# Spreading the auxiliary matmuls of a transformer block over its score units, with zero products in the idle TensorE time, a leaner prologue and tail, and softmax sums inverted in a 128x16 tile

## The chip, the cores and the metric

The kernel runs on one core of one Trainium2 chip. The metric is the device time of one execution in microseconds (us). A profiled execution also has a "span", from its first to its last instruction, which is about 2 us shorter than its time.

A core has five engines that matter here. TensorE (PE in the profile) multiplies matrices and writes to PSUM, of which the kernel uses eight banks of 512 fp32 columns. ScalarE (ACT) does the exponentials, VectorE (DVE) and GpSimd (POOL) do elementwise work, and SyncE (SP) issues most DMA transfers. Each engine runs its own list of instructions in order, and engines wait for each other by semaphores.

## The reference, cut to what matters

The computation is one block: a modulated layernorm, attention with 32 heads, a second modulated layernorm, and an MLP that begins with a layernorm of its own. S = 2048 rows, D = 640, head dimension 20, F = 1536, bf16.

```python
mod = (_silu(c) @ w_mod).reshape(c.shape[0], 6, 1, -1)      # sa, ca, ga, sb, cb, gb
h = _layernorm(x) * (1 + ca) + sa
    q, k, v = ...(h @ wqkv)                                  # 32 heads of 20
    scores = einsum('bhqd,bhkd->bhqk', q, k) * Dh ** (-0.5)
    p = softmax(scores)                                      # 32 x 2048 x 2048 exponentials
    o = einsum('bhqk,bhkd->bhqd', p, v)
x = x + ga * (o @ wo)
h = _layernorm(x) * (1 + cb) + sb
    y = _layernorm(h)
    h = _gelu(einsum('bsd,df->bsf', y, w1) + b1)
    ... einsum('bsf,fd->bsd', h, w2) + b2
x = x + gb * (...)
```

The 134 million exponentials are what bounds the kernel: at 128 lanes they are 694 ACT instructions, 661 of them 128x1536.

## The kernel before

The kernel is a Python program that lists operations, and a small list scheduler inside it that decides the order on each engine. The scheduler has a model of time (`dur`, `lat`, a DMA bandwidth). It chooses the operation that is ready first by this model, and by priority among those that are ready. The order is then fixed in the program: on the chip nothing is reordered.

The query rows are cut in four chunks of 512, the heads in 8 groups of 4. One "score unit" is three score matmuls into three PSUM banks, and one exp over them. Units alternate between banks 0 to 2 and 3 to 5; bank 6 takes the products with V. So **one bank, number 7, is left for everything else** in the steady part: projections of later groups, softmax sums, output projection and MLP of the previous chunk. I call these auxiliary matmuls.

```python
def score_unit(ts, b0, prio=1):            # three matmuls into banks b0..b0+2, then one exp
    ...
    P.op("pe", em, R=R, W=[pb], ..., prio=prio, mode="r", name="qk")
    acts.append(P.op("act", lambda e: e.activation(dst, src, ACTF.Exp, scale=SCALE), ...))   # L587

def proj_job(g, which, tc, prio, rel, eng):
    bb = bank(aux_bank())
    for kt in range(KD):                   # all five become available at the same exp, `rel`
        mm(bb, wqk[:, kt, which, ...], hT[:, kt, ...], kt == 0, kt == KD - 1, prio, 512, rel=rel, name="proj")
    ...

def sel_job(qc, g, rel, prio=6):           # softmax sums of a group of four heads
    bb = bank(aux_bank())
    d = ot[:, qc % 2, g, :]
    mm(bb, selz, d, True, True, prio, 512, rel=rel, name="sel")       # row of sums -> all rows of its head
    dve(lambda e: e.reciprocal(rinv, bb), [bb], [rinv], 512, ...)     # L616, 128x512
    dve(lambda e: e.tensor_tensor(d, d, rinv, op=ALU.mult), ...)      # L617

# prologue
dve(lambda e: e.memset(wqk, 0.0), [], [wqk], KD * 2 * NG * 128, mode=2)     # L441
dve(lambda e: e.memset(va_flat, 1.0), [], [va_flat], TT * H * VW, mode=2)   # L442
...                                        # four steps of 512 rows: layernorm, transpose, project, all of V,
...                                        # and the scores of head group 0
row_mod(gab, wm1, 0, None); row_mod(sbr, wm1, D, None); ...                 # then row modulations and wo scaling
# tail, per 128 rows
normalize(hdst, x2[:, tl, :], tt, 3)
dve(lambda e: e.tensor_tensor(hdst, hdst, cb1, op=ALU.mult), ..., eng=eng)  # eng = "pool", L820
dve(lambda e: e.tensor_tensor(hdst, hdst, sbr, op=ALU.add), ..., eng=eng)   # L822
```

The softmax here doesn't subtract the row's maximum and nothing guards it: scores larger than these inputs give would overflow.

Of the kernel before, what the change touches and what calls it, by code (L numbers as in the profile page):

```python
# [6 lines left out]
ALU = mybir.AluOpType  # L7
# [6 lines left out]
class Op:  # L14
    __slots__ = ("eng", "emit", "strong", "weak", "dur", "lat", "prio", "rel", "idx",
                 "users", "dma", "nbytes", "name", "npred", "ready", "t0", "t1",
                 "inc", "cnt", "sem", "startusers", "mode", "order")


class Sched:  # L20
# [7 lines left out]
    NDSEM = 40  # L28

    def __init__(self, nc, es):  # L30
        self.nc = nc
        self.ops = []
        self.lw = {}
        self.rd = {}
        self.fp = {}
        self.sem = {e: es.enter_context(nc.semaphore("s_" + e))
                    for e in ("pe", "act", "dve", "pool")}
        self.dsem = [es.enter_context(nc.semaphore(f"dm{i}")) for i in range(self.NDSEM)]
        self.ndma = 0
        self.dlast = [None] * self.NDSEM  # L40
# [35 lines left out]
    def op(self, eng, emit, R=(), W=(), dur=0.1, lat=None, prio=5, rel=None, name="",  # L76
           dma=False, nbytes=0, mode=0, after=()):
        o = Op()
        o.eng, o.emit, o.dur, o.prio, o.rel, o.name = eng, emit, dur, prio, rel, name
        o.lat = dur if lat is None else lat  # L80
        o.dma, o.nbytes, o.mode = dma, nbytes, mode
        o.idx = len(self.ops)
# [37 lines left out]
    def schedule(self):  # L120
# [4 lines left out]
        for o in ops:  # L125
            for i in o.strong | o.weak:
                ops[i].users.append(o.idx)
                o.npred += 1
            if o.rel is not None:
                o.rel.startusers.append(o.idx)  # L130
                o.npred += 1
# [5 lines left out]
        bw = 0.0  # L137
        for o in ops:
            if o.npred == 0:
                avail[o.eng].append(o)  # L140
        left = len(ops)
        while left:
# [6 lines left out]
            assert be is not None, "deadlock"  # L149
            cand = [x for x in avail[be] if x.ready <= bt + 1e-9]  # L150
# [4 lines left out]
            if be == "pe" and lastmode[be] != o.mode:  # L155
                d += 0.05
                lastmode[be] = o.mode
            free[be] = bt + d
            if o.dma:
                s = max(bt + 1.4, bw)  # L160
                bw = s + o.nbytes / 260e3
                o.t1 = bw + 0.8
            else:
                o.t1 = bt + (d - o.dur) + o.lat
# [98 lines left out]
def bass_adaLN_cond__mha_block__mixer_channel_mlp__prompt_kernel(  # L263
# [6 lines left out]
    NG, TT, NQC, KD, KF = 8, 16, 4, 5, 12  # L270
# [3 lines left out]
    VW, RING = 24, 15  # L274

    es = ExitStack()
    with es:
# [28 lines left out]
        o_qT = alloc(NQC * NG * 512 * 2)  # L306
# [9 lines left out]
        qT = V(o_qT, [NQC, NG, 512])  # L316
# [5 lines left out]
        ring = V(o_ring, [RING, 512])  # L322
# [11 lines left out]
        raw = V(o_qT + 8192, [KD, 3 * D])  # L334
        wm0 = V(o_ring, [KD, 2 * D])
        wm1 = V(o_qT + 8192, [KD, 2 * D])
        wm2 = V(o_kT + 4 * S * 2, [KD, 2 * D])
        xb = [V(o_wo, [4, D]), V(o_wo + 5120, [4, D]), V(o_mlp, [4, D])]
        hn1 = V(o_kT + 2 * S * 2, [6, D])
        ident = V(alloc(256), [128])  # L340
        selz = V(alloc(256), [128])
        rinv = V(alloc(2048), [512], F32)
        gbb2 = V(alloc(1280), [D])
        sbr = V(alloc(1280), [D])
        cb1 = V(alloc(1280), [D])
        gbh = V(o_mlp + 5120, [D])
        gab = V(o_mlp + 6400, [D])
        b2b = V(o_kT + S * 2, [D])
        st6 = [V(alloc(64), [2, 6], F32) for _ in range(6)]
        st2 = V(alloc(TT * 64), [TT, 16], F32)  # L350
        c_row = V(alloc(256), [128])
        b1row = V(alloc(256), [128])
        small = V(alloc(64), [16], F32)
# [6 lines left out]
        sbl = V(o_kT + S * 2 + 1280, [KD, 128])  # L360
        ones = V(o_kT + S * 2 + 2560, [128])
# [6 lines left out]


        def c_pe(n):  # L370
            return n / 2400.0

        def act(outp, inp, func, R=(), W=None, n=512, prio=5, name="", **kw):
            d = n / 1200.0 + 0.082
            return P.op("act", lambda e: e.activation(outp, inp, func, **kw),  # L375
                        R=[inp] + list(R), W=[outp], dur=d, lat=d + 0.22, prio=prio, name=name)

        def dve(emit, R, W, n, mode=1.0, prio=5, name="", extra=0.0, eng="dve"):
            d = 0.06 + n / (960.0 * mode) + extra
            if eng == "pool":  # L380
                d = 0.1 + n / 800.0 + extra
            return P.op(eng, emit, R=R, W=W, dur=d, lat=d + 0.12, prio=prio, name=name)

        def dma(eng, o_, i_, nbytes, prio=5, name=""):
            return P.op(eng, lambda e: e.dma_start(o_, i_), R=[i_], W=[o_], dur=0.6 if eng != "pool" else 1.0,
                        dma=True, nbytes=nbytes, prio=prio, name=name)

        def mm(outp, lhsT, rhs, start, stop, prio, n, mode="f", rel=None, tp=None, name="", R=None):
            kw = {} if tp is None else dict(tile_position=tp)
            return P.op("pe", lambda e: e.matmul(outp, lhsT, rhs, start=start, stop=stop, **kw),  # L390
                        R=[lhsT, rhs] if R is None else R, W=[outp], dur=c_pe(max(n, 64)),
                        lat=c_pe(max(n, 64)) + 0.15, prio=prio, mode=mode, rel=rel, name=name)

        def tr(outp, inp, idn, prio, n=128, rel=None, name=""):
            return P.op("pe", lambda e: e.transpose(outp, inp, idn), R=[inp, idn], W=[outp],  # L395
                        dur=c_pe(n), lat=c_pe(n) + 0.15, prio=prio, mode="f", rel=rel, name=name)

        banks = [[0, 1, 2, 3, 4, 5, 6, 7], 0]
# [8 lines left out]


# [3 lines left out]
        def xsrc(tc):  # L412
            return X2[tc * 512:(tc + 1) * 512, :].rearrange("(t p) d -> p t d", p=128)

        cv = c[0]
        dma("sp", c_row[0:KD, :], cv.rearrange("(kt p) -> kt p", p=128), 1280)
        dma("sp", xb[0][:, 0:2, :], xsrc(0)[:, 0:2, :], 327680)
        dma("sp", xb[0][:, 2:4, :], xsrc(0)[:, 2:4, :], 327680)
        dma("act", wm0[:, :, 0:D], wmod_v[:, :, 0:D], 819200, prio=0)
        dma("act", wm0[:, :, D:2 * D], wmod_v[:, :, D:2 * D], 819200, prio=0)  # L420
        dma("sp", raw[:, :, D:2 * D], wqkv_v[:, :, D:2 * D], 819200)
        dma("sp", raw[:, :, 0:D], wqkv_v[:, :, 0:D], 819200)
        dma("sp", wv[:], wqkv_v[:, :, 2 * D:3 * D], 819200)
        dma("sp", xb[1][:], xsrc(1), 655360)
        dma("sp", xb[2][:], xsrc(2), 655360)
# [4 lines left out]
        def pool(emit, W, n, R=(), prio=5, name=""):  # L430
            return dve(emit, list(R), list(W), n, prio=prio, name=name, eng="pool")

        pool(lambda e: e.memset(ident, 0.0), [ident], 128)
        pool(lambda e: e.affine_select(out=ident, in_=ident, compare_op=ALU.not_equal, fill=1.0,
                                       base=0, pattern=[[-1, 128]], channel_multiplier=1),
             [ident], 128, R=[ident])
        pool(lambda e: e.memset(ones, 1.0), [ones], 128)
        pool(lambda e: e.memset(negh, -0.5), [negh], 16)
        wqk_k = wqk[:, :, 1, :]
        wqk_q = wqk[:, :, 0, :]  # L440
        dve(lambda e: e.memset(wqk, 0.0), [], [wqk], KD * 2 * NG * 128, mode=2)  # L441
        dve(lambda e: e.memset(va_flat, 1.0), [], [va_flat], TT * H * VW, mode=2)  # L442


        b = aux_bank()
        tb = bankh(b)
        tr(tb[:, 0:KD], c_row[0:KD, :], ident[0:KD, 0:KD], 0, 16)
        act(t_col, tb[:, 0:KD], ACTF.Tanh, n=KD, scale=0.5, prio=0)
        dve(lambda e: e.tensor_copy(c_col, tb[:, 0:KD]), [tb[:, 0:KD]], [c_col], KD, prio=0)
        dve(lambda e: e.tensor_scalar(t_col, t_col, 0.5, 0.5, op0=ALU.mult, op1=ALU.add),  # L450
            [t_col], [t_col], KD, prio=0)
        dve(lambda e: e.tensor_tensor(s_col, t_col, c_col, op=ALU.mult), [t_col, c_col], [s_col], KD, prio=0)  # L452

        def mod_cols(wm, base, blocks, prio, rel=None):

            bb = bank(aux_bank())
            for m in blocks:
                for kt in range(KD):
                    mm(bb[:, m:m + 1], wm[:, kt, (m - base) * 128:(m - base + 1) * 128],
                       s_col[:, kt:kt + 1], kt == 0, kt == KD - 1, prio, 100, rel=rel)  # L460
            m0, m1 = blocks[0], blocks[-1] + 1
            dve(lambda e: e.tensor_copy(modc[:, m0:m1], bb[:, m0:m1]), [bb[:, m0:m1]], [modc[:, m0:m1]],
                m1 - m0, prio=0)

        mod_cols(wm0, 0, list(range(0, 10)), 0)
        dve(lambda e: e.tensor_scalar_add(modc[:, 5:10], modc[:, 5:10], 1.0), [modc[:, 5:10]],
            [modc[:, 5:10]], 5, prio=0)


        def pad_copy(which, kt, eng):  # L470
            dst = wqk[:, kt, which, :].rearrange("p (h i) -> p h i", i=32)[:, :, 0:DH]
            src = raw[:, kt, which * D:(which + 1) * D].rearrange("p (h i) -> p h i", i=DH)
            if eng == "act":
                act(dst, src, ACTF.Copy, n=D, prio=3)
            else:
                dve(lambda e: e.tensor_copy(dst, src), [src], [dst], D, eng=eng, prio=6)

        for kt in range(KD):
            pad_copy(1, kt, "act" if kt % 2 == 0 else "pool")
        for kt in range(KD):  # L480
            pad_copy(0, kt, "act" if kt % 2 == 0 else "pool")


        def stats(xt, tt, si, prio):
            s6 = st6[si]
            s2 = st2[:, tt, 0:2]
            for hf in range(2):
                xi = xt[:, hf * 320:(hf + 1) * 320]
                dve(lambda e, hf=hf, xi=xi: e.bn_stats(s6[:, hf, :], xi), [xi], [s6[:, hf, :]], 400, prio=prio)  # L489
            dve(lambda e: e.bn_aggr(s2, s6), [s6], [s2], 30, extra=0.06, prio=prio)  # L490

        def rstd(t0, n, prio):
            v = st2[:, t0:t0 + n, 1]
            r = st2[:, t0:t0 + n, 2]
            pool(lambda e: e.tensor_scalar_add(r, v, 1e-5), [r], 4, R=[v], prio=prio)  # L495
# [474 lines left out]
```

## Time and profile before

| | before |
|---|---|
| median time | 1132.8 us |
| span of the profiled execution | 1127.9 us |
| ACT busy | 977.9 us, of which exp 933.2 |
| first exp / first 1536-wide exp | 33.3 / 97.9 us |
| last exp ends | 1058.8 us |
| mean granted TensorE clock | 0.796 |

First some lines of the page: the busy time of each engine (share of the span, number of instructions), the granted TensorE clock in 40 equal slices (tenths of full speed), the chain of work that ended last (shares of the span), and three groups of instructions (busy us, mean ns of one, then idle time of the engine just before them and what ended most of it).

```profile
PE 864.7 (77%) x5675; PEld 263.7 (23%) x5740; DVE 414.6 (37%) x577; ACT 977.9 (87%) x766; POOL 138.7 (12%) x165
...
PEclk9998999899577687578678776588667687688759
...
ACT 59%; PE 30%; DVE 6%; POOL 4%; issue 1%; another core or an unknown queue 0%; POOLq 0%; DVEq 0%
...
L587 ACT ACTIVATE arena<-psum 128x1536 bf16<-128x1536 f32 (+2 forms) x694 | 933.2, 1481 | 64.3 <-PE psum L578 63.4
...
L390 PE MATMUL psum<-arena 128*128 128x320 bf16 (+2 forms) x1417 | 353.3, 378 | 49.6 <-DVE arena L452 17.3
...
L616 DVE RECIPROCAL arena<-psum 128x512 f32<-128x512 f32 x32 | 107.4, 3355 | 20.1 <-PE psum L578 15.3
```

ACT bounds the kernel, and PE is the only engine it really waits for. The 128x512 reciprocals take 3.36 us each on DVE.

Next the ACT timeline: start, length in us, the instruction and how many in a row, and in brackets the idle time before it and what ended that.

```profile
33.32 1.94 ACT L587 ACTIVATE arena<-psum 128x1024 bf16<-128x1024 f32 x2 [0.20 <-PE psum L578]
...
97.88 2.79 ACT L587 ACTIVATE arena<-psum 128x1536 bf16<-128x1536 f32 x2 [17.64 <-PE psum L578]
101.09 1.45 ACT L587 ACTIVATE arena<-psum 128x1536 bf16<-128x1536 f32 x1 [0.41 <-PE psum L578]
103.76 1.45 ACT L587 ACTIVATE arena<-psum 128x1536 bf16<-128x1536 f32 x1 [1.22 <-PE psum L578]
...
107.79 45.89 ACT L587 ACTIVATE arena<-psum 128x1536 bf16<-128x1536 f32 x34 [0.95 <-PE psum L578]
...
1097.41 1.02 ACT L375 ACTIVATE arena<-psum 128x1024 bf16<-128x1024 bf16 x1 [38.56 <-PE psum L395]
```

Where nothing is missing, 34 exps take 45.89 us, so 1.35 us each (1.347 from one start to the next). The 661 exps of this size and 18 tanh of 0.94 us make about 907 us, which no part of this change touches. The rest of the 1128 us lies in the prologue (the 17.64 us gap, and five exps that limp up to 107.8), in waits of the steady part, and in the tail (the 38.56 us gap and the MLP after it).

The waits of ACT for score matmuls between 125 and 1035 us (total, number, longest, in us), and the granted clock (the column after POOL) in stretches of 141 us:

```profile
ACT arena L587 <- PE psum L578: 41.0, 68, 1.5
```

```profile
141.00:282.00 141.00, 120.39 (x823) 34.00 (x839) 53.05 (x59) 139.37 (x104) 0.00 (x0) 0.98 0.02 6
282.00:423.00 141.00, 108.44 (x697) 28.43 (x705) 53.33 (x75) 133.75 (x100) 39.80 (x40) 0.70 0.08 28
```

In the first whole stretch PE has 120 us of work and is granted 0.98; from 282 us on it has about 108 and is granted 0.70 to 0.77. The Trainium skill, "TensorE: Matmul & The Clock Gate", Part 1, describes this: by default the clock is throttled to half, and activity over windows of 3413 ns releases it. The trace agrees: its clock records from 32 us on hold only 1.0 and 0.5, all but the last in multiples of 3.413 us, so that a figure like 0.70 is a mean of full and half clock. So the fullest stretch for PE runs it the fastest. (The first 141 us, with 103 us of work and 0.96, are no counterexample: the first 32 us, in which PE does little, have no clock record and count as full.)

### The profile page before, as it was taken

How to read it: one execution, taken by the hardware profiler on the slowest of the kernel's cores; microseconds unless marked ns; L12 is line 12 of the kernel's file. 1: busy time of each engine (PE TensorE's matmuls, PEld its weight loads, DVE VectorE, ACT ScalarE, POOL GpSimd, SP SyncE). 2: the span in 40 equal slices, each digit the busy share in tenths (PEclk: the TensorE clock that was granted, in tenths of full speed). 3: DMA queues.
4: the chain of work that ended last, by engine and by line, in shares of the span. 5: the costliest groups of instructions: out<-in, count | busy, mean ns of one | idle time of the engine just before them, and what ended most of it. 6: DMA issues, size and time to landing. Idle time of an engine off the chain costs nothing.

```text
span 1127.9 us, 13029 instructions
## 1 busy us (share of the span) xinstructions
PE 864.7 (77%) x5675; PEld 263.7 (23%) x5740; DVE 414.6 (37%) x577; ACT 977.9 (87%) x766; POOL 138.7 (12%) x165
## 2 busy tenths in 40 slices
PE   1997888888787768777787777877787877777818
PEld 1442222222122211122222211122122211122305
DVE  8722434333234354322034444322233444322361
ACT  2874999999999999999999998999989999999502
POOL 2124000000524100000024100000025000000080
PEclk9998999899577687578678776588667687688759
DMA  8110000000300000000000000000000000000000
GB/s 287 75 30 1 1 1 1 24 2 2 139 1 1 1 1 1 24 6 12 6 1 1 1 1 1 24 11 8 6 1 1 1 1 1 24 12 6 6 1 24
DMA packets 14259, 20.99 MB, mean 19 GB/s; under 512 B 634, under 2 KB 12282, under 8 KB 14202
## 3 DMA queue, kind: packets, MB, share of 16 engines
q1 hardware_dynamic: 12890, 18.52, 4.9%
q10 hardware_dynamic: 1312, 1.64, 0.5%
q8 instruction: 45, 0.74, 0.3%
q14 instruction: 12, 0.10, 0.0%
HBM read 17.54 MB, written 2.62 MB: 18 GB/s over the span
## 4 chain that ended last, share of the span: by engine, by line
ACT 59%; PE 30%; DVE 6%; POOL 4%; issue 1%; another core or an unknown queue 0%; POOLq 0%; DVEq 0%
ACT arena L587 57%; PE psum L390 16%; PE psum L578 8%; PE psum L603 5%; DVE arena L616 1%; ACT arena L375 1%; DVE arena L442 1%; PE psum L395 1%; POOL arena L787 1%; POOL arena L820 1%; POOL arena L827 1%; DVE arena L489 1%; POOL arena L822 1%; POOL arena L496 1%; DVE arena L809 0%
## 5 line engine op out<-in xcount | busy, mean ns | idle before, releaser
L587 ACT ACTIVATE arena<-psum 128x1536 bf16<-128x1536 f32 (+2 forms) x694 | 933.2, 1481 | 64.3 <-PE psum L578 63.4
L578 PE MATMUL psum<-arena 32*128 32x512 bf16 x2048 | 321.5, 463 | 175.6 <-ACT arena L587 170.1
L390 PE MATMUL psum<-arena 128*128 128x320 bf16 (+2 forms) x1417 | 353.3, 378 | 49.6 <-DVE arena L452 17.3
L603 PE MATMUL psum<-arena 128*32 128x512 bf16 x2048 | 247.0, 473 | 3.7 <-DVE arena L610 3.7
L390 PEld LDWEIGHTS psum<-arena 128*128 128x128 bf16 x1482 | 128.7, 107 | 230.7 <-issue 118.8
L578 PEld LDWEIGHTS psum<-arena 32*128 32x128 bf16 x2048 | 68.5, 93 | 428.1 <-ACT arena L587 352.7
L616 DVE RECIPROCAL arena<-psum 128x512 f32<-128x512 f32 x32 | 107.4, 3355 | 20.1 <-PE psum L578 15.3
L495 POOL TENSOR_SCALAR arena<-arena 128x1 f32<-128x1 f32 (+1 forms) x40 | 10.1, 252 | 710.5 <-DVE arena L490 710.1
L603 PEld LDWEIGHTS psum<-arena 128*32 128x32 bf16 x2048 | 54.2, 96 | 161.8 <-issue 151.2
L540 DVE CAST arena<-psum 128x512 bf16<-128x512 f32 x60 | 41.5, 691 | 117.7 <-PE psum L390 114.5
L875 DVE SCALAR_TENSOR_TENSOR arena<-psum,arena 128x320 bf16<-128x320 f32 x32 | 15.7, 492 | 182.7 <-PE psum L390 182.6
L847 DVE TENSOR_SCALAR arena<-psum,arena 128x512 bf16<-128x512 f32 x36 | 27.0, 751 | 101.4 <-PE psum L390 101.4
L610 DVE CAST arena<-psum 128x512 bf16<-128x512 f32 x32 | 22.0, 688 | 101.0 <-PE psum L603 100.9
L375 ACT ACTIVATE arena<-psum 128x320 bf16<-128x320 f32 (+3 forms) x22 | 10.7, 496 | 44.4 <-PE psum L395 38.6
L489 DVE BATCH_NORM_STATS2 arena<-arena 128x6 f32<-128x320 bf16 x96 | 43.5, 481 | 15.2 <-POOL arena L822 14.4
L395 PE MATMUL psum<-arena 128*128 128x128 bf16 (+2 forms) x162 | 19.3, 271 | 31.5 <-DVE arena L499 28.1
L809 DVE TENSOR_TENSOR arena<-psum,arena 128x320 bf16<-128x320 f32 x32 | 15.1, 489 | 75.2 <-PE psum L390 75.1
L888 POOL TENSOR_TENSOR arena<-arena 128x640 bf16<-128x640 bf16 x12 | 16.3, 1400 | 197.7 <-DMA arena<-in_B_w_dram 197.7
L499 DVE TENSOR_SCALAR arena<-arena 128x640 bf16<-128x640 bf16 x48 | 27.3, 584 | 25.3 <-POOL arena L496 25.2
L375 ACT ACTIVATE arena<-arena 128x1024 bf16<-128x1024 bf16 (+1 forms) x24 | 23.8, 1007 | 8.9 <-DMA arena<-in_A_wqkv_dram 8.9
L375 ACT ACTIVATE arena<-psum,arena 128x512 bf16<-128x512 bf16 (+1 forms) x24 | 17.3, 741 | 15.5 <-PE psum L395 10.7
L858 DVE SCALAR_TENSOR_TENSOR arena<-arena 128x1024 bf16<-128x1024 bf16 x18 | 21.9, 1217 | 22.6 <-ACT arena L375 22.4
(42 smaller groups left out, 232.5 us busy)
## 6 DMA issues: line engine op xcount, KB each, us to landing
arena<-in_A_x_dram SPq DMA_DIRECT2D x7, 640.0 KB, 4.2
arena<-in_B_w_dram SPq DMA_DIRECT2D x2, 1920.0 KB, 10.2
arena<-in_w_mod_dram SPq DMA_DIRECT2D x2, 1600.0 KB, 10.2
out_dram<-arena SPq DMA_DIRECT2D x16, 160.0 KB, 1.8
arena<-in_A_wqkv_dram SPq DMA_DIRECT2D x3, 800.0 KB, 11.2
arena<-in_w_mod_dram ACTq DMA_DIRECT2D x2, 800.0 KB, 7.2
arena<-in_A_wo_dram SPq DMA_DIRECT2D x4, 200.0 KB
arena<-in_A_x_dram SPq DMA_DIRECT2D x2, 320.0 KB, 6.5
```

The lines of the kernel that those rows point to most:

```text
L375: return P.op("act", lambda e: e.activation(outp, inp, func, **kw), R=[inp] + list(R), W=[outp], dur=d, lat=d + 0.22, prio=prio, name=name)
L390: return P.op("pe", lambda e: e.matmul(outp, lhsT, rhs, start=start, stop=stop, **kw), R=[lhsT, rhs] if R is None else R, W=[outp], dur=c_ ...
L395: return P.op("pe", lambda e: e.transpose(outp, inp, idn), R=[inp, idn], W=[outp], dur=c_pe(n), lat=c_pe(n) + 0.15, prio=prio, mode="f", r ...
L489: dve(lambda e, hf=hf, xi=xi: e.bn_stats(s6[:, hf, :], xi), [xi], [s6[:, hf, :]], 400, prio=prio)
L499: dve(lambda e: e.tensor_scalar(dst, xt, st2[:, tt, 0:1], st2[:, tt, 2:3], op0=ALU.subtract, op1=ALU.mult), [xt, st2[:, tt, 0:3]], [dst], ...
L540: dve(lambda e: e.tensor_copy(d, bb), [bb], [d], 512, prio=2)
L578: r = e.matmul(o_, lh, rh, start=True, stop=True, tile_position=(32 * hl, 0))
L587: acts.append(P.op("act", lambda e: e.activation(dst, src, ACTF.Exp, scale=SCALE), R=[pb], W=[dst], dur=d, lat=d + 0.24, prio=4, name="exp"))
L603: r = e.matmul(o_, lh, rh, start=(kt == 0), stop=(kt == TT - 1), tile_position=(0, 32 * hl))
L610: dve(lambda e: e.tensor_copy(d, bank(6)), [bank(6)], [d], 512, prio=0, name="pvcopy")
L616: dve(lambda e: e.reciprocal(rinv, bb), [bb], [rinv], 512, extra=2.8, prio=3, name="recip")
L847: dve(lambda e: e.tensor_scalar(d, bb, b1col[:, ft:ft + 1], None, op0=ALU.add), [bb, b1col], [d], 512, prio=2, name="m1ev")
```

## The change

The intent has four parts.

1. **Prologue.** The memsets touch only what has to be set; the q and k weights of head group 0 are loaded first; only a quarter of V is made, and the rest of V and the row modulations move under the exps of chunk 0.
2. **Steady part.** The matmuls of one auxiliary job become available one by one, at different score units (`Pace`). The scheduler also inserts zero products (zero weights, added to bank 6 where they change nothing) where its model of PE is idle and has streamed fewer than 3500 columns in the last 3.413 us.
3. **Softmax sums.** The 4x512 sums of a group go by DMA into a 128x16 tile, are inverted there, go to DRAM and come back as a broadcast. This replaces 31 of the 32 large reciprocals.
4. **Tail.** The second layernorm runs on ACT and DVE instead of POOL, and most of the output projection is summed before the last group is ready.

The diff also retunes the scheduler's own model: the assumed DMA rate goes from 260 to 350 GB/s, and PE's assumed time now doubles after a window with little PE work.

The diff, cut to its core:

```diff
+            if be == "pe" and self.filler is not None and gate and bt > free["pe"] + 0.06:
+                f0 = free["pe"]
+                while fl and fl[0][0] < f0 - self.TICK:      # TICK = 3.413
+                    fl.pop(0)
+                if sum(x[1] for x in fl) < self.fill_min:    # fill_min = 3500 columns
+                    o = self.op("pe", self.filler[0], ..., name="fill", wc=float(self.filler[1]))
...
+        P.filler = (lambda e: e.matmul(bank(6), zero, idr, start=False, stop=False, ...), 512)
...
+            def rels(self, n):                               # class Pace
+                return [self.u0 + int(self.slot + self.span * i / n) for i in range(n)]
...
-            for kt in range(KD):
-                mm(bb, wqk[...], hT[...], kt == 0, kt == KD - 1, prio, 512, rel=rel, name="proj")
+            mmjob(bb, [(wqk[...], hT[...]) for kt in range(KD)], 512, prio, pace, "proj")
...
+        def sum_job(ci, g):
+            P.op("sp", lambda e: e.dma_start(dst, row), R=[d], W=[sumt], ..., nbytes=4096)       # L716
+            dve(lambda e: e.reciprocal(r_, s_), [s_], [r_], 16, dur=0.2, prio=3, name="recip")   # L718
+            o = P.op("sp", lambda e: e.dma_start(flat_, r_), R=[r_], ..., nbytes=8192)           # L720
+            src = bass.AP(tensor=scr.tensor, offset=k * 2048, ap=[[n, 4], [0, 32], [1, n]])
+            P.op("sp", lambda e: e.dma_start(rb, src), W=[rb], ..., nbytes=262144, after=[o])    # L723
+            dve(lambda e: e.tensor_tensor(d, d, rb, op=ALU.mult), [d, rb], [d], n, ..., name="div")  # L724
...
-        dve(lambda e: e.memset(wqk, 0.0), [], [wqk], KD * 2 * NG * 128, mode=2)
-        dve(lambda e: e.memset(va_flat, 1.0), [], [va_flat], TT * H * VW, mode=2)
+        pool(lambda e: e.memset(wqk32[:, :, 10:16], 0.0), ...)
+        dve(lambda e: e.memset(va32[:, :, 10:12], 1.001937866210937500), ...)
...
-        pool(lambda e: e.memset(wo_pad, 0.0), [wo_pad], NG * D)
+        pool(lambda e: e.memset(wo_pad, 0.0), [wo_pad], dur=4.4, prio=7)                         # L868, runs at 29.65 us; in the old kernel at 57.2
...
-            ln2(pq, tl)
+            ln2(ci, tl, tail=True)             # normalize on ACT, products on DVE
+        early = [(tl, half) for tl in range(min(nt, 3)) for half in range(2)]
```

## The prediction

It was written from the reference, the code before, the diff and the profile before, with nothing built.

> **What bounds it now.** The exp activations of L587 on ACT. By groups they are busy 933 of 1127.9 us; the chain gives ACT 59%. The ACT timeline shows the pace when nothing is missing: 32 exps of 128x1536 in 43.2 us, 1.35 us each. 661 of them make about 890 us and 18 tanh in between (0.94 us each) 17 us: 907 us that this change does not touch. The rest, about 221 us, is what can shrink:
> - Prologue: the first exp starts at 33.3 us (DVE spent 14.6 us on two memsets before its first statistics at 19.0). Head group 0 lasts to 80.2 with PE 93 to 99% busy. Then ACT idles 17.6 us while the row modulations and the wo scaling run, and limps until 107.8, having done 5 large exps.
> - Steady part: ACT waited 41 us for score matmuls (68 waits between 125 and 1035 us). The granted clock is 0.98 at 141 to 282 us, then 0.70 to 0.77. The waits follow runs of 3 to 8 auxiliary matmuls of 0.33 to 0.43 us each in front of a score unit.
> - Tail: 69 us from the last exp's end (1058.9). The second layernorm, with 12 POOL products of 1.39 us in the chain, holds the MLP back to 1098.
>
> **What the change does.**
> 1. Prologue: smaller memsets, q/k weights of group 0 loaded first, only a quarter of V made there, row modulations and the rest of V moved under the exps. First exp at about 19 us; each of the four steps falls from about 12 us to about 10.3 (then ACT, 9.7 us of work); group 1 follows at once. The steady part starts near 60 instead of an effective 101 (107.8 less 5 exps): -41 us.
> 2. Steady part: auxiliary matmuls come one at a time, and zero products keep PE active. The Trainium skill, "TensorE: Matmul & The Clock Gate", Part 1, says activity releases the clock; the trace agrees so far, as the densest stretch had 0.98. I expect over 0.93 throughout, and PE waits of ACT near 10 us, not 41. The first chunk takes on V and row work; its second group is the tight one.
> 3. Softmax sums: 31 of 32 reciprocals (3.36 us each) leave DVE, but three DMAs in sequence replace each. The broadcast's outer dimension of 4 limits it to 4 DMA engines by the skill's "DMA: Bandwidth & Descriptors", Rules for kernel authors. DVE, in order, will wait 1 to 2 us for some; with one auxiliary bank, that reaches PE: +8 us estimated.
> 4. Tail: ACT and DVE replace the POOL products, output-projection sums are started early: -11 us; the MLP's last 30 us stay.
>
> **Sum.** 60 + 907 + 18 + 58 = 1043 us span; the times run about 4 us above the span. Predicted 1048 us, range 1022 to 1085. Faster by over 2%: 0.94; within 2%: 0.05; slower: 0.01.
>
> **What would show it.** First exp near 19 us, first 1536-wide exp near 60; no ACT gap over 3 us up to 1000 us; granted clock over 0.93 in all 141 us stretches; ACT's waits for score matmuls 10 to 20 us; DVE waits on DMA at the small reciprocal and the product after it; MLP start within 30 us of the last exp.
>
> **What would make it wrong.** The zero products may be too few, or placed by the schedule's own model where the chip is not idle, so the clock stays near 0.75 or they delay scores: ACT would still wait 40 us (about 1070). DMA waits on DVE of over 3 us per group would add 30. V in the first chunk could overload PE and give back 10 to 15 us. On the other side, if every wait disappears, about 1025.

## More of the kernel before

The unchanged kernel took 1127 to 1134 us on the chips of the experiments, and 1132.6 to 1137.2 us on the first chip.

A long pause is not needed for the clock to fall: between 282 and 987 us no wait of PE is over 1.9 us, and the clock is halved in 45 spells.

## The result, and the profile after

The changed kernel took 1063.0 us in the median of 4 runs (1059.5 to 1065.9), against 1132.8. The ratio is 0.937 (95% interval 0.933 to 0.941). Ratios here and below are the mean time of one kernel's fast runs over that of the other's in the same rounds, so not quite the ratio of the medians that I quote.

The same lines of the page for the changed kernel, with the zero products (L507) and the product with the inverse sums (L724) added:

```profile
PE 870.6 (82%) x6139; PEld 275.8 (26%) x6139; DVE 316.7 (30%) x595; ACT 970.2 (92%) x752; POOL 135.6 (13%) x173
...
PEclk9899999999968989988889999788899899897769
...
ACT 62%; PE 24%; DMA 7%; DVE 5%; POOL 1%; issue 1%; SPq 0%; POOLq 0%
...
L663 ACT ACTIVATE arena<-psum 128x1536 bf16<-128x1536 f32 (+2 forms) x694 | 931.2, 1569 | 22.1 <-PE psum L653 20.7
...
L507 PE MATMUL psum<-arena 128*128 128x512 bf16 x269 | 97.4, 444 | 0.0
...
L724 DVE TENSOR_TENSOR arena<-arena 128x512 bf16<-128x512 bf16 x31 | 23.8, 767 | 108.6 <-DMA arena<-scr 108.6
```

The exps cost the same (931 against 933 us). What fell is ACT's idle time before them, from 64.3 to 22.1 us. PE now spends 97 us on products with zero. DMA enters the chain with 7%.

The ACT timeline: the first exp, the largest gap of the prologue, the first 1536-wide exp, and the start of the MLP.

```profile
22.98 5.60 ACT L663 ACTIVATE arena<-psum 128x1024 bf16<-128x1024 f32 x6
...
37.38 1.45 ACT L414 ACTIVATE arena<-psum,arena 128x512 bf16<-128x512 bf16 x2 [5.63 <-PE psum L436]
...
67.50 42.41 ACT L663 ACTIVATE arena<-psum 128x1536 bf16<-128x1536 f32 x31 [0.49 <-PE psum L653]
...
1028.86 1.02 ACT L414 ACTIVATE arena<-psum 128x1024 bf16<-128x1024 bf16 x1 [1.34 <-PE psum L436]
```

The waits between 68 and 1000 us, and the granted clock in stretches of 141 us:

```profile
DVE arena L724 <- DMA arena<-scr: 108.6, 31, 11.3
...
DVE arena L718 <- DMA arena<-arena: 36.2, 20, 6.0
...
ACT arena L663 <- PE psum L653: 19.4, 25, 3.0
```

```profile
141.00:282.00 141.00, 127.66 (x916) 40.39 (x915) 41.52 (x65) 138.80 (x103) 1.31 (x1) 1.00 0.08 25
282.00:423.00 141.00, 113.71 (x763) 31.43 (x762) 47.74 (x86) 132.43 (x100) 39.73 (x40) 0.86 0.08 27
```

The later stretches were granted 0.86 to 0.92, where before they had 0.70 to 0.77.

To see where the time went I cut each profiled execution at three points: the start of the 1536-wide exps, the end of the last exp, and the end. "Lost" is the length of the middle part less the 907 us of its ACT work.

| us | before | after | change |
|---|---|---|---|
| start of the 1536-wide exps | 97.9 | 67.5 | -30.4 |
| middle part (lost) | 961.0 (54.0) | 930.9 (23.9) | -30.1 |
| from the last exp's end | 69.1 | 60.8 | -8.3 |
| span | 1127.9 | 1059.2 | -68.7 |

The first five of the large exps of "before" took the 9.9 us up to 107.79, where 6.7 would have done. These 3 us stand in the middle part here; the prediction counted them to the start (an effective 101).

The trace shows four kinds of delay that remain, each with an instance.

**A memset on POOL holds up DVE.** In the prologue, at 29.8 us (the timeline of all engines):

```profile
29.65 4.36 POOL L868 MEMSET arena<- 128x5120 bf16 x1
29.76 5.49 DVE L562 TENSOR_SCALAR arena<-arena 128x640 bf16<-128x640 bf16 x4
...
37.38 1.45 ACT L414 ACTIVATE arena<-psum,arena 128x512 bf16<-128x512 bf16 x2 [5.63 <-PE psum L436]
```

Four normalizations take 5.49 us, where two of them take 0.80 us at 9.31 us; the transposes behind them come late, and ACT waits 5.63 us. The Trainium skill, "SBUF — State Buffer", "SBUF: two separate sides", says that DVE and GpSimd share a port pair, that an instruction which uses it holds it to its end, and that the other engine blocks meanwhile. The lines fit this.

**DVE waits for the broadcast, in order, and PE for DVE.** At 167 us:

```profile
167.31 0.69 DVE L724 TENSOR_TENSOR arena<-arena 128x512 bf16<-128x512 bf16 x1 [2.82 <-DMA arena<-scr]
167.92 0.65 DVE L618 CAST arena<-psum 128x480 bf16<-128x480 f32 x1
...
168.63 0.82 PE L430 MATMUL psum<-arena 128*128 128x512 bf16 x3 [1.46 <-DVE arena L618]
...
169.82 2.79 ACT L663 ACTIVATE arena<-psum 128x1536 bf16<-128x1536 f32 x2 [1.45 <-PE psum L653]
```

The product L724 needs the broadcast. Behind it stands the cast L618, which empties the only auxiliary bank. PE waits for the bank with a score unit queued behind, and ACT waits for the score unit. In a quiet stretch the broadcast was issued at 72.40 and the product started at 77.23, so 4.8 us; the scheduler's model has 1.4 us, 0.26 MB at 350 GB/s and 0.6 us, so 2.75. From 74.5 to 76.0 us, at its height, DMA moved 102 to 106 GB/s with 0.26 to 0.27 of the 16 engines busy. The Trainium skill, "DMA: Bandwidth & Descriptors", "Rules for kernel authors", says that a transfer whose outermost dimension is c below 16 is confined to at most c engines; here it is 4, and about a quarter of 16 is what the trace shows.

**The small transfers before the broadcast stand behind 3.9 MB of weights.** The loads of w1 and w2 are issued at 275.98 and 277.17 us, the 4 KB copy of the sums at 276.41, and the next two transfers of this group only at 284.19 and 290.69. The broadcast itself, from 290.69 to 295.47, took its usual 4.8 us. DVE waits 11.3 us, PE 3.51 and ACT 3.04:

```profile
295.47 1.11 DVE L724 TENSOR_TENSOR arena<-arena 128x512 bf16<-128x512 bf16 x1 [11.31 <-DMA arena<-scr]
...
296.73 0.42 PE L430 MATMUL psum<-arena 128*128 128x320 bf16 x1 [3.51 <-DVE arena L724]
...
298.17 4.26 ACT L663 ACTIVATE arena<-psum 128x1536 bf16<-128x1536 f32 x3 [3.04 <-PE psum L653]
```

**Zero products at half clock.** At 340 us, where the granted clock is 0.50 (339 to 345 us), four of them take 1.89 us; at full clock they were planned at 0.21 each, and the scores behind them come late:

```profile
340.40 1.89 PE L507 MATMUL psum<-arena 128*128 128x512 bf16 x4
...
342.88 2.79 ACT L663 ACTIVATE arena<-psum 128x1536 bf16<-128x1536 f32 x2 [0.93 <-PE psum L653]
```

### The profile page after: what moved, and what is told of

The parts are those of the page before. It is cut to its first block, busy times and chain, and to the rows that moved or that the text cites. A ratio compares the mean times of both kernels' runs of the same rounds, so it can differ in the third digit from the quotient of the medians.

```text
span 1059.2 us, 14000 instructions
## 1 busy us (share of the span) xinstructions
PE 870.6 (82%) x6139; PEld 275.8 (26%) x6139; DVE 316.7 (30%) x595; ACT 970.2 (92%) x752; POOL 135.6 (13%) x173
## 4 chain that ended last, share of the span: by engine, by line
ACT 62%; PE 24%; DMA 7%; DVE 5%; POOL 1%; issue 1%; SPq 0%; POOLq 0%
ACT arena L663 61%; PE psum L430 11%; PE psum L653 6%; PE psum L680 4%; DMA arena<-scr 3%; PE psum L507 2%; DMA scr<-arena 2%; ACT arena L414 1%; DMA arena<-arena 1%; DMA arena<-in_A_x_dram 1%; DVE arena L544 1%; DVE arena L562 1%; DVE arena L602 1%; DVE arena L618 1%; DVE arena L724 1%
## 5 line engine op out<-in xcount | busy, mean ns | idle before, releaser
L663 ACT ACTIVATE arena<-psum 128x1536 bf16<-128x1536 f32 (+2 forms) x694 | 931.2, 1569 | 22.1 <-PE psum L653 20.7
L653 PE MATMUL psum<-arena 32*128 32x512 bf16 x2048 | 292.3, 417 | 128.8 <-ACT arena L663 123.8
L430 PE MATMUL psum<-arena 128*128 128x512 bf16 (+3 forms) x1611 | 354.1, 329 | 32.6 <-DMA arena<-in_w_mod_dram 6.2
L680 PE MATMUL psum<-arena 128*32 128x512 bf16 (+1 forms) x2048 | 220.4, 422 | 0.4
L430 PEld LDWEIGHTS psum<-arena 128*128 128x128 bf16 x1611 | 125.9, 100 | 209.1 <-issue 104.2
L507 PE MATMUL psum<-arena 128*128 128x512 bf16 x269 | 97.4, 444 | 0.0
L680 PEld LDWEIGHTS psum<-arena 128*32 128x32 bf16 (+1 forms) x2048 | 51.5, 93 | 133.3 <-issue 127.9
L414 ACT ACTIVATE arena<-arena 128x1024 bf16<-128x1024 bf16 (+2 forms) x28 | 31.8, 1138 | 29.6 <-POOL arena L558 21.8
L724 DVE TENSOR_TENSOR arena<-arena 128x512 bf16<-128x512 bf16 x31 | 23.8, 767 | 108.6 <-DMA arena<-scr 108.6
L982 POOL TENSOR_TENSOR arena<-arena 128x640 bf16<-128x640 bf16 x12 | 16.8, 1432 | 148.3 <-DMA arena<-in_B_w_dram 148.3
L688 DVE CAST arena<-psum 128x512 bf16<-128x512 f32 x32 | 22.1, 692 | 44.1 <-PE psum L680 43.8
L915 POOL TENSOR_TENSOR arena<-arena 128x640 bf16<-128x640 bf16 x24 | 33.4, 1393 | 7.4 <-DVE arena L562 7.4
L507 PEld LDWEIGHTS psum<-arena 128*128 128x128 bf16 x269 | 22.2, 104 | 41.2 <-issue 34.9
```

What stands on the lines that cost most here:

```text
L414: return P.op("act", lambda e: e.activation(outp, inp, func, **kw), R=[inp] + list(R), W=[outp], dur=d, lat=d + 0.2, prio=prio, name=name)
L430: return P.op("pe", lambda e: e.matmul(outp, lhsT, rhs, start=start, stop=stop), R=[lhsT, rhs], W=[outp], dur=d, lat=d + 0.17, prio=prio, ...
L507: P.filler = (lambda e: e.matmul(bank(6), zero, idr, start=False, stop=False, skip_group_check=True), 512)
L653: r = e.matmul(o_, lh, rh, start=True, stop=True, tile_position=(32 * hl, 0))
L680: r = e.matmul(o_, lh, rh, start=(kt == 0), stop=(kt == TT - 1), tile_position=(0, 32 * hl))
L688: dve(lambda e: e.tensor_copy(d_, acc), [acc], [d_], n, prio=0, name="pvcopy")
```

## The experiments

There were 12 kernels, all correct. My theory was that spreading, zero products and the softmax sums each buy a part of the middle's gain, that their gains add, and that the miss against the prediction comes from the delays just listed. The rivals were that one part (above all the zero products, by the clock) carries the gain and the others ride on it, and that the visible waits cost nothing because another limit stands behind them. Each experiment edits the changed kernel. "us" is the median; "ratio" is to the kernel before in the same rounds.

### Undoing one part of the steady part at a time

**nofill**: the zero products are planned, so every order stays the same, but not emitted.

```diff
-                    ins = o.emit(eng)
+                    ins = None if o.name == "fill" else o.emit(eng)
```

> The changed kernel with the 269 zero products left out and the order of everything else untouched (L507 gone). Theory (they keep the clock up and so pay): mean granted clock falls from 0.905 to below 0.85, ACT's waits for score matmuls rise from 21 us to over 30 us, time 1072 to 1085 us. Rival (the one-by-one order alone removed the waits; in stretches of low clock the zero products themselves stand in front of score units, as before 340, 386, 561 and 665 us): clock falls, but the waits stay near 21 us or fall, time 1055 to 1066 us.

Measured: 1075.5 us, ratio 0.953 (0.950 to 0.956), mean clock 0.802; 0.71 to 0.78 in the stretches from 282 us on. ACT's waits for scores rose from 19.4 to 26.0 us, in 49 places:

```profile
282.00:423.00 141.00, 116.06 (x719) 28.45 (x717) 45.87 (x84) 135.56 (x102) 39.83 (x40) 0.71 0.11 38
```

```profile
ACT arena L663 <- PE psum L653: 26.0, 49, 2.4
```

Clock and time came as the theory had it; the waits stayed under the 30 us that it expected. The view of waits leaves out gaps under 0.15 us; with these, the idle time before the exps rose from 22.1 to 31.8 us, and the middle part lost 12.5 us more. The zero products are worth 0.9529 - 0.9374 = 0.0155 of 1130 us, 17 us. They are what raises the clock, but without them the kernel is still 4.7% under the one before: the clock does not carry the whole gain.

**bunch**: all matmuls of one auxiliary job become available at its first unit again.

```diff
-                return [self.u0 + int(self.slot + self.span * i / n) for i in range(n)]
+                return [self.u0 + int(self.slot)] * n
```

> The changed kernel with each auxiliary product's 5 to 12 matmuls released together again, zero products kept. Theory (spreading is what removed the waits): runs of 3 to 8 auxiliary matmuls return in front of score units, ACT's waits for them go from 21 us to 35 to 50 us, time 1075 to 1092 us. Rival (the clock is what mattered, and zero products hold it): waits stay under 27 us, time within 6 us of 1063 us.

Measured: 1072.2 us, ratio 0.949 (0.945 to 0.953), clock 0.895, ACT's waits for scores 33.1 us in 42 places:

```profile
ACT arena L663 <- PE psum L653: 33.1, 42, 2.9
```

Waits and time both lie a little under what the theory expected (35 to 50 us, 1075 to 1092 us), and above the rival's. Spreading is worth 13 us, at an almost equal clock. With the edit the scheduler made a new order, with 320 zero products in place of 269 (282 in oldsum), so these runs differ from the changed kernel in a little more than the one edit.

**oldsum**: the 128x512 reciprocals from PSUM are back in place of the DMA chain.

```diff
-            add(UG * g + 2, 0.1, lambda pace, g=g: sum_job(0, g))
+            add(UG * g + 3, 0.1, lambda pace, g=g: sel_job(0, g, pace))       # and so in the other chunks
```

> The changed kernel with the sums of 31 head groups inverted in 128x512 on DVE from the auxiliary bank again (3.36 us each), no DMA round trip. Theory (the DMA path frees DVE and the bank and pays): DVE busy rises by about 100 us, ACT's waits rise by 5 to 15 us, time 1066 to 1080 us. Rival (what the reciprocals held up is replaced by DVE's in-order waits for the broadcast, 108.6 us in 31 waits, so the two are worth the same): within 4 us of 1063 us, the wait of 3 us at 295 us gone.

Measured: 1081.8 us, ratio 0.956 (0.954 to 0.959), clock 0.906, DVE busy 413 us. The DMA chain is worth 21 us, the largest of the three and more than I had expected. Most of it is lost in chunk 0, which has taken on V and the row work: from 108 to 317 us ACT is busy 187.6 us (the column before POOL), against 201.3 in the changed kernel, but from 317 to 800 us 474.3 against 473.3.

```profile
108.00:317.00 209.00, 181.18 (x1321) 60.56 (x1321) 79.09 (x94) 187.61 (x140) 18.20 (x15) 0.97 0.07 23
```

The longest waits of ACT are there. This one follows a reciprocal, which holds the one auxiliary bank for 3.36 us; four zero products (1.89 us) and ten auxiliary matmuls also stand between the two, so the wait is not the reciprocal's alone:

```profile
219.32 3.36 DVE L699 RECIPROCAL arena<-psum 128x512 f32<-128x512 f32 x1 [0.59 <-PE psum L430]
...
228.54 2.79 ACT L663 ACTIVATE arena<-psum 128x1536 bf16<-128x1536 f32 x2 [4.99 <-PE psum L653]
```

**steadyold**: the three edits together.

> The changed kernel with all three changes of the steady part undone at once: no zero products, auxiliary matmuls released in bunches, sums inverted in 128x512. Undone one at a time they cost about 17, 13 and 21 us against the changed kernel (51 in all). Theory A (each removes its own waits, so they add): ratio to the kernel before near 0.98, about 1110 us. Theory B (they guard the same slack, and the steady part of before lost only 27 us more than that of the changed kernel): ratio 0.955 to 0.97, 1080 to 1095 us.

Measured: 1113.9 us, ratio 0.987 (0.985 to 0.988), clock 0.787, ACT's waits for scores 63.4 us in 69 places, longest 6.6. Undoing all three costs 0.0492 of 1130 us, 56 us; the three single costs add up to 17 + 13 + 21 = 51. So they nearly add, within the intervals, as theory A had it, and none of them merely rides on another. The 56 us are more than the 30 us by which the middle part improved over the kernel before. The middle lost 75.9 us here, against 54.0 in the kernel before, and the stretch that is mostly chunk 0 holds all of the difference: from 108 to 317 us ACT is busy 182.5 us here and was 207.4 before.

```profile
108.00:317.00 209.00, 172.56 (x1239) 58.49 (x1261) 77.29 (x91) 182.48 (x136) 14.10 (x10) 0.93 0.06 21
```

I read this as the work that the new prologue moved under the exps of chunk 0, which the old steady part could not hide. The traces show where the time goes; no run takes that work out of chunk 0 again.

### The prologue and the tail

No run puts the old prologue back: that it brought 30 us is read from the two profiles alone.

**memset**: the memset of `wo_pad` on POOL is cut into eight pieces, of 32-bit elements, so that the whole is shorter, too.

```diff
-        pool(lambda e: e.memset(wo_pad, 0.0), [wo_pad], dur=4.4, prio=7)
+        wo32 = V(o_wo, [NG, D // 2], F32)
+        for g in range(NG):
+            pool(lambda e, g=g: e.memset(wo32[:, g, :], 0.0), [wo32[:, g, :]], dur=0.4, prio=7)
```

> The changed kernel with the 4.4 us POOL memset of the padded wo cut into eight of 32-bit elements, same place in the program. Theory (the long POOL instruction keeps DVE's four normalizations, 5.49 us at 29.8 us, from running, and ACT idles 5.6 us at 31.7): the four take about 1.6 us, the gap shrinks to under 2 us, the first large exp starts near 63 instead of 67.5 us, time 1057 to 1061 us. Rival (DVE was waiting for something else, such as the row statistics' POOL steps): gap and time unchanged, within 2 us of 1063 us.

Measured: 1056.9 us, ratio 0.936 (0.933 to 0.938).

```profile
30.08 1.28 POOL L870 MEMSET arena<- 128x320 f32 x4
30.17 2.42 DVE L562 TENSOR_SCALAR arena<-arena 128x640 bf16<-128x640 bf16 x4
...
34.31 1.45 ACT L414 ACTIVATE arena<-psum,arena 128x512 bf16<-128x512 bf16 x2 [2.14 <-PE psum L436]
```

The normalizations took 2.42 us instead of 5.49, the gap shrank from 5.63 to 2.14 us, and the 1536-wide exps began at 63.1 instead of 67.5. The other four pieces had been placed between 9.9 and 13.5 us. So the long memset did hold DVE up: with less of it in the way the normalizations and the gap became shorter, though not as short as I had expected (1.6 us and under 2 us). Of the 4.4 us only about 2 arrived in the ratio, which is within the intervals: the middle part was re-ordered too, and lost 28.2 us instead of 23.9 in the profiled execution.

**oldtail**: the second layernorm of the last chunk is back on POOL, no early sums, one large reciprocal.

```diff
-            ln2(ci, tl, tail=True)
+            ln2(ci, tl)
...
-        early = [(tl, half) for tl in range(min(nt, 3)) for half in range(2)]
+        early = []
...
-        sel_job(ci, NG - 1, prio=1, step=128)
+        sel_job(ci, NG - 1, prio=1)
```

> The changed kernel with the end as before: second layernorm with POOL products and DVE normalization, output-projection sums not started early, last sums inverted in one piece. Theory (my prediction put the tail's gain at 11 us; the profiles give 69.0 us from the last exp's end before and 60.8 after): time 8 to 10 us over the changed kernel (ratio 0.945 to 0.947 to before), the tail near 69 us. Rival (the shorter tail comes from the one bank of 2.8 us of wo matmuls that stood in front of the last PV before, and not from the engines): only 2 to 4 us.

Measured: 1073.3 us, ratio 0.950 (0.948 to 0.952); I had expected 0.945 to 0.947. The tail took 69.6 us instead of 60.8, so 8.8 us, as between the two original kernels. The whole cost is 0.0124 of 1130 us, 14 us. The middle part was also 6 us longer (937.4), although the edit touches nothing there but what the scheduler makes of it; whether that is another order or the spread from run to run (the changed kernel itself varies by 6 us) stays open.

### What the remaining waits cost

**wload**: the two weight loads are issued 11 and 31 units into chunk 1 rather than at its start.

```diff
-        dma("sp", w1[:], B_w1.rearrange("(kt p) f -> p kt f", p=128), 1966080)
-        dma("sp", w2[:], B_w2.rearrange("(ft p) d -> p ft d", p=128), 1966080)
+        k0 = len(acts)                      # the same two loads, with rel=k0 + 11 and rel=k0 + 31
```

> The changed kernel with the loads of the two MLP weights (1.9 MB each) issued about 15 and 42 us into the second query chunk instead of beside the sums of the last group of the first. Theory (the 3.0 us ACT gap at 295 us came from the sum's DMAs queued behind 3.8 MB; DVE waited 11.3 us, PE 3.5): the gap is gone, DVE's longest wait for the broadcast falls to under 5 us, time 2 to 4 us less. Rival (another wait takes its place, or the loads collide with later sums): no gap over 2 us less, time unchanged.

Measured: 1058.5 us, ratio 0.937 (0.936 to 0.939). The 3 us gap of ACT is gone (its longest wait is 1.3 us), but the ratio is the same as the changed kernel's. DVE's longest wait for the broadcast fell from 11.3 to 8.4 us, not under 5 as expected. This leaves it open whether the wait had a price: the middle part lost 3.3 us less in the profiled execution, as the theory would have it, but the interval of the changed kernel's ratio alone is 4.5 us to either side, so the ratio can neither show nor exclude 3 us. The clock of its runs, 0.895 to 0.901, was slightly lower than the changed kernel's 0.900 to 0.914.

**dlat**: the scheduler's model is told that the broadcast is longer. The instructions are the same; their order changes.

```diff
-            ... dma=True, nbytes=262144, after=[o])
+            ... dma=True, nbytes=960000, after=[o])      # 1.4 + 960000/350e3 + 0.6 = 4.7 us in the model
```

> The changed kernel with the time that its static order assumes for the broadcast DMA raised from 2.75 us to about 4.75 us, which is what the trace has from issue to the product after it (72.40 to 77.23 us). No instruction is added or removed, only DVE's product is placed later. Theory (DVE in order waits 2 to 3 us for most broadcasts and holds the one auxiliary bank): DVE's waits for the broadcast fall from 108.6 us to under 60 us, ACT's waits by 3 to 6 us, time 3 to 6 us less. Rival (those waits fall in DVE's spare time and cost nothing): waits fall, time within 2 us.

Measured: 1050.6 us, ratio 0.930 (0.929 to 0.932), clock 0.923 in the profiled run. DVE's waits for the broadcast fell from 31 to 16 and from 108.6 to 66.9 us (I had expected under 60), and ACT's waits for scores to 10.3 us. So a wrong latency in the model cost 8 us, more than the 3 to 6 that I had expected. But with the order of DVE the order on PE and the places of the zero products changed as well.

**dlate**: to separate these, only DVE's list is touched. After scheduling, each product that needs a broadcast is moved behind the DVE operations of the next 2.1 us of model time, if nothing needs it before. Every other engine's list is identical to the changed kernel's.

```diff
-        self.tend = max(o.t1 for o in ops)
+        self.tend = max(o.t1 for o in ops); div_later(self.ops, self.streams["dve"])
```

> The changed kernel with one thing moved: on DVE, the product that follows each broadcast stands 1 to 3 places later (up to 2.1 us of the order's own time), behind evacuations of the auxiliary bank. Every other engine's program, zero products included, is the same, line for line. The run with the longer assumed DMA time gained 8 us (ratio 0.9303 against 0.9374), but it also reordered PE. Theory (DVE's in-order wait for the broadcast, ahead of an evacuation, was the cost): most of that gain is here too, ratio 0.930 to 0.934, DVE's waits for the broadcast fall from 108.6 us to under 70 us. Rival (the other run gained from a luckier PE order or better placed zero products): ratio 0.936 to 0.939.

Measured: 1055.8 us, ratio 0.934 (0.932 to 0.937), clock 0.897 in the profiled run. DVE waits 16 times for the broadcast, as in dlat. Where the changed kernel stalled at 169.82, ACT now runs through:

```profile
158.70 13.99 ACT L663 ACTIVATE arena<-psum 128x1536 bf16<-128x1536 f32 x10
...
165.22 0.66 DVE L618 CAST arena<-psum 128x480 bf16<-128x480 f32 x1 [2.06 <-PE psum L430]
165.82 0.69 DVE L724 TENSOR_TENSOR arena<-arena 128x512 bf16<-128x512 bf16 x1
```

The cast now comes first, and the product waits for nothing. This bought 0.0031 of 1130 us, 3.5 us, and the interval overlaps the changed kernel's. The ratio falls between what the theory (0.930 to 0.934) and the rival (0.936 to 0.939) expected. By the means, the in-order wait of DVE is less than half of what dlat gained. The other 4.5 us belong to what dlat changed beside it, PE's order or where the zero products fall; these were not separated.

### Putting the remedies together

**fix**: memset, dlat and wload together, and a longer assumed time for the small q and k loads, meant to move other work ahead of the DVE wait at 16.31 us.

```diff
-            dma("act", raw0[:, w, :, :], wqkv_v[:, :, w * D:w * D + 80], 102400, prio=0)
+            dma("act", raw0[:, w, :, :], wqkv_v[:, :, w * D:w * D + 80], 600000, prio=0)   # model only
```

> A version meant to beat both kernels: the changed kernel with the memset in eight pieces, the MLP weight loads later, the true broadcast time in the static order, and a longer assumed time for the two small strided q/k loads (so that DVE doesn't wait 3 us for the second x tile ahead of the first tile's evacuation). Single runs gave -2, 0 and -8 us by ratio and -4 us at the start of the large exps. If the parts add: first exp near 21 us, first large exp near 61 us, steady stretch 915 to 920 us, time on this chip 1040 to 1047 us, ratio 0.920 to 0.927. If they guard the same slack: no better than 0.930.

Measured: 1044.9 us, ratio 0.925 (0.923 to 0.927), clock 0.908, ACT's waits for scores 8.7 us in 17 places. The last part failed: DVE still waits 2.83 us for the second block of x at 16.33, because the edit moved the weight copies and not this, and the first exp came later, at 24.3 us. The ratio lies in the range expected if the parts add (0.920 to 0.927).

**fixd**: the same with more zero products.

```diff
-        self.fill_min = 3500
+        self.fill_min = 4600
```

> The same version with more zero products (added while fewer than 4600 instead of 3500 columns were streamed in the last 3.4 us of the order's own time). Theory (granted clock still drops to 0.86 to 0.92 in chunks 1 to 3, and cold stretches are where the last waits are): clock over 0.95, ratio 0.004 to 0.008 below that of the version with 3500. Rival (the extra zero products stand in front of score units and cost what the clock gives): ratio equal or higher, ACT's waits equal or more.

Measured: 1037.9 us, ratio 0.919 (0.917 to 0.921), mean clock 0.967. There are 564 zero products in place of 265. The stretch of the earlier windows view:

```profile
282.00:423.00 141.00, 119.28 (x834) 35.17 (x832) 53.31 (x90) 137.47 (x105) 39.43 (x40) 0.95 0.10 28
```

No stretch up to 987 us is under 0.95, and the time fell by another 0.0059 of 1130 us, 7 us. Twice as many useless products cost less than the clock gives; ACT's waits fell to 6.6 us in 9 places.

**best**: as fixd, but in place of the failed edit the scheduler is told that the V weights arrive later, which puts the waiting statistics behind the first tile's work.

```diff
-        dma("sp", wv[:], wqkv_v[:, :, 2 * D:3 * D], 819200)
+        dma("sp", wv[:], wqkv_v[:, :, 2 * D:3 * D], 1800000)      # model only
```

> The last version without its failed part (the longer assumed time of the small q/k loads put the weight copies behind the first transposes on ACT: first exp at 25.8 us instead of 23.0) and with the V weight load's assumed time longer instead, which only puts the first tile's two evacuations on DVE ahead of the second tile's statistics. Memset in pieces, later MLP loads, true broadcast time and 4600 columns as in the version that gave 0.9188. If DVE's wait of 2.8 us for the second x tile was what held the first tile back: DVE's evacuation at 15 instead of 17.1 us, first exp near 21 us, first large exp at 60 to 62 us, ratio 0.914 to 0.918. If another wait bounds the prologue (group 0 takes 40 us from the first exp whatever its start): first large exp near 63 us, ratio 0.918 to 0.921.

Measured: 1040.1 us in the median of 5, ratio 0.920 (0.918 to 0.922). The first exp came at 19.8 us instead of 23.0, and the 1536-wide exps began at 61.2. But the time is the same as fixd's within the intervals, which could not show 2 us, and of the two ratios expected it met the higher one, that for another wait bounding the prologue (0.918 to 0.921), though with the start at 61.2 and not near 63. The version is 8% under the kernel before and 1.8% under the changed one (0.9201 / 0.9374 = 0.9815).

All profiled executions, cut as above:

| us | start | middle (lost) | tail | clock |
|---|---|---|---|---|
| before | 97.9 | 961.0 (54.0) | 69.1 | 0.796 |
| after | 67.5 | 930.9 (23.9) | 60.8 | 0.905 |
| nofill | 66.5 | 943.4 (36.4) | 61.4 | 0.802 |
| bunch | 67.1 | 948.3 (41.3) | 59.6 | 0.895 |
| oldsum | 66.3 | 948.9 (41.9) | 59.9 | 0.906 |
| steadyold | 66.7 | 982.9 (75.9) | 61.8 | 0.787 |
| memset | 63.1 | 935.2 (28.2) | 60.6 | 0.910 |
| oldtail | 66.6 | 937.4 (30.4) | 69.6 | 0.905 |
| wload | 67.7 | 927.5 (20.5) | 60.7 | 0.895 |
| dlat | 67.5 | 919.0 (12.0) | 61.9 | 0.923 |
| dlate | 68.2 | 925.0 (18.0) | 62.9 | 0.897 |
| fix | 62.5 | 919.8 (12.8) | 60.6 | 0.908 |
| fixd | 63.6 | 914.4 (7.4) | 60.4 | 0.967 |
| best | 61.2 | 913.2 (6.2) | 60.0 | 0.962 |

These are single executions; differences of a few us in the middle part between kernels are not resolved by this table alone.

## Why the prediction was right or wrong

The verdict (faster by over 2%, chance 0.94) and the range (1022 to 1085 us) held; the number was 15 us too low (1048 against 1063). The sum, term by term, for the span:

| term | predicted | measured |
|---|---|---|
| start of the 1536-wide exps | 60 | 67.5 |
| ACT's own work, unchanged | 907 | 907 (taken) |
| lost in the middle | 18 | 23.9 |
| tail | 58 | 60.8 |
| span | 1043 | 1059.2 |

1. **Bound by the exps: right.** The exp group is busy 933 and 931 us, and every gain is a gap of ACT that closed.
2. **Prologue: the mechanism right, the size off by 7.5 us**, the largest term of the miss. The first exp came at 22.98, not 19, and there was a gap of 5.63 us. I had costed the operations one by one and not what stands next to them: a POOL memset that blocks DVE for 3 us, and a DVE wait of 3.01 us for the second block of x in front of the first tile's evacuation. The one run with both mended (best) starts at 61.2, with the first exp at 19.8, close to the prediction.
3. **Zero products raise the clock: right, but not to "over 0.93 throughout".** It was 0.86 to 0.92 from 282 us on. The step that failed is that I took the change's threshold of 3500 columns as enough; "too few" stood among the risks, but I had not used it in the sum. With 4600 (fixd) all stretches up to 987 us have 0.95 or more and the time falls by 7 us. The effect itself is shown by nofill: 17 us.
4. **ACT's waits for scores of 10 to 20 us: right** (19.4). I had put them together from 10 us of ordinary waits and 8 us from the DMA chain. With the broadcast's latency told to the scheduler the middle loses 12.0 us, and the time falls by 8 us. That this is my 8 us is in part luck: more than half of it came not from DVE's wait as I had argued (dlate gains 3.5 us) but from what the scheduler rearranged with it. No ACT gap over 3 us: wrong, by the 5.63 us gap and one of 3.04 us behind the weight loads, which I had not seen coming; wload, which removes this second one, does not resolve what it cost.
5. **DMA waits of over 3 us per group would add 30 us: wrong.** They were 108.6 us over 31 groups for the broadcast, 3.5 us each, and 36.2 us more for the small copy. DVE has idle time (busy 30%), and most of these waits never reached ACT, whose waits for scores were 19.4 us in all.
6. **V in the first chunk could give back 10 to 15 us: it did not**, as long as all three parts of the steady change were there. From 141 to 282 us ACT was busy 138.8 of 141 us, at a clock of 1.00. From 108 to 317 us it was busy 201.3 us; with the old sums alone 187.6, and with all three parts undone 182.5. So the crowded chunk was a real danger, and most of what the DMA chain is worth shows there.
7. **The tail's 58 us: 60.8**, and oldtail measures the gain of the tail itself as 8.8 us where I had 11. The MLP began 30.5 us after the last exp's end; I had expected within 30.
8. **The time above the span**: I added 4 to 5 us and it is 2 (1061.15 against 1059.2 in the profiled run), which hid 2 to 3 us of the miss. The 4 us came from setting the span of one execution (1127.9 us; its own time was 1129.66) against the median of others (1132.8).

Open are the 4.5 us that dlat gains beyond dlate, the 6 us of the middle part in oldtail, and whether the 3 us gap and the last 2 us of start cost time at all, which the runs do not resolve.

## What to carry to other kernels

When one engine bounds a kernel and another feeds it, look at what stands in line in front of the feed: one long instruction on the only free buffer, a run of side matmuls, or an in-order wait for a DMA can each delay it, and here their fixes nearly added up. When a static scheduler decides the order, measure the latencies it assumes; two constants that it had too low (a broadcast of 4.8 us planned at 2.75, and a fill threshold of 3500 columns) cost 8 and 7 us here, with no change to the useful work. And before moving work under a bounded stretch, make sure that this stretch can hide it: the new prologue and tail with the old steady part kept only about a fifth of the gain (ratio 0.987 instead of 0.937).

## What the Trainium skill lacked or had wrong

- "TensorE: Matmul & The Clock Gate" (Part 1) says that activity releases the clock, and gives the 3413 ns window, but of how much activity keeps it only that the throttle returns after an idle window. Here the kernel before was at 0.70 to 0.77 from 282 to 987 us with no wait of PE over 1.9 us. From 282 us on, zero products added below 3500 planned columns in 3.413 us gave stretches of 0.86 to 0.92, below 4600 they gave 0.95 to 1.00 in fixd and 0.92 to 1.00 in best, and none gave 0.71 to 0.78. Zero weights count as activity.
- No page that I found says that spending PE time on zero products can pay in a kernel bound by another engine: 269 products of 97 us in all bought 17 us, and 564 instead of 265 bought 7 us more.
- "DMA: Bandwidth & Descriptors" (Rules for kernel authors) was right on the engines of a broadcast with outer dimension 4. The page lists a bandwidth per engine, but no measured time of such a transfer: 4.8 us from issue to use for 256 KB, at 106 GB/s at its height.
- "SBUF — State Buffer" (SBUF: two separate sides) was right that DVE and GpSimd block each other, but has no such case with its size: a 4.36 us memset on GpSimd stretched four normalizations to 5.49 us; with the memset in pieces they took 2.42 us.
